# The v loads of three attention units, issued by GpSimd instead of the sync engine

## The chip, the core and the metric

The kernel runs on one core of one Trainium2 chip. The metric is the device time of one execution in microseconds; runs are given by their median.

## The reference

q, k and v have the shape (4, 8, 576, 64): batch, heads, sequence, head size. Attention is computed in chunks of 64 positions, each with itself alone. Its output goes through two MLPs; the result is float32.

```python
scores = scale * np.matmul(q_c, k_c.transpose(0, 1, 2, 4, 3))
attn = softmax(scores)
x = np.matmul(attn, v_c)                  # as (2304, 512)
x = ((x @ w_a) * (x @ w_b)) @ w_out       # 512 -> 1536 -> 512
h = x @ w_in                              # 512 -> 2048
P = a[0] + a[1] * h + a[2] * h**2 + a[3] * h**3
Q = 1.0 + abs(b[0]) * abs(h) + abs(b[1]) * h**2
out = (P / (Q + 1e-06)) @ w_out2          # 2048 -> 512
```

The weights arrive as 64-bit floats. The kernel loads each weight tile as it is (512 KB) and makes float32 of it on ScalarE and VectorE, in four pieces.

## The kernel before

The 2304 tokens are cut into 18 units of 128 (two chunks of 64, eight heads). A unit's attention runs in named pieces: `k` and `q` transpose the loaded k and q on TensorE (L359) and copy them out on ScalarE (L361); `S` makes the scores (L381), takes their maximum and subtracts it on VectorE (L386, L387); `X` is the exponential on ScalarE (L391); `E` normalizes on VectorE; `P` transposes the result (L407); `V` multiplies it with v (L425) and writes the upper part of x (`x_hi`); `L` makes the lower part (`x_lo`, L437). Matmuls are done as three products of such upper and lower parts (L275 to L277).

The kernel then goes through three stages: the gated product of the first MLP (first for units 0 to 2, while the other units' attention is woven in between; later for the rest), the product with `w_out`, and the second MLP with the rational function.

The order of everything is written out by hand. Two strings set the start: LOADS (L81) the DMAs and FIRST (L80) the compute pieces. A letter and a digit are a tensor or piece and its unit, `w` is the next weight tile or the next quarter of its conversion, `d` a few extra matmuls with the identity (L935), `+` a load.

```python
FIRST = "k0 q0 w w d2 S0 w X0 w k1 E0 d2 q1 S1 w X1 P0 k2 w q2 E1 V0 w S2 ...".split()
LOADS = "k0 q0 w k1 q1 w v0 k2 q2 v1 w w v2 k3 q3 k4 q4".split()
```

Each engine runs its instructions in program order. Loads are issued by the sync engine (SP), one after another; the stores of intermediate results go through GpSimd (POOL), whose first work is to make the identity matrix `ident` for the transposes. A load of q, k or v for a unit is 128 partitions by 8 heads by 64 floats: 1024 pieces of 256 bytes in the source, 256 KB in all. q, k and v of a unit up to unit 5 lie in one tile, `kqv`. Unit 0 to UH - 1 = 2 are the first three units, whose x the first gated matmuls read.

Of the kernel before, what the change touches and what calls it, by code (L numbers as in the profile page):

```python
# [20 lines left out]
def chunk_attention_two_mlps(  # L21
# [34 lines left out]
    nc = tc.nc  # L56
# [18 lines left out]
    UH = GH // P  # L75
# [248 lines left out]
    def a_load(u, *names):  # L324

        if u >= NU:
            return
        (b0, c0), (b1, c1) = CHUNKS[u]
        for nm, src in (("k", k), ("q", q), ("v", v)):
            if nm not in names:  # L330
                continue
            if u < 2 * UH:
                if ("raw", u) not in un:
                    un["raw", u] = p_X.tile([P, 3, H, D], F32, name="kqv", tag=f"X{NQ - 1}_{u + 1}")
                t = un["raw", u][:, "kqv".index(nm)]
            elif u % 2 and nm != "v":
                if nm == "k":
                    un["odd"] = p_X.tile([P, 3, H, D], F32, name="kq", tag=f"X{NQ - 1}_7")
                t = un["odd"][:, "kq".index(nm)]
            else:  # L340
                t = p_qk.tile([P, H, D], F32, name=nm, tag=nm, bufs=2 if nm == "v" else 1)
            if b0 == b1:
                parts = [(t, src[b0, :, c0 * CH:(c0 + 2) * CH, :])]
            else:
                parts = [
                    (t[c * CH:(c + 1) * CH], src[bb, :, cc * CH:(cc + 1) * CH, :])
                    for c, (bb, cc) in enumerate(((b0, c0), (b1, c1)))
                ]
            for dst, s in parts:
                nc.sync.dma_start(out=dst, in_=s.rearrange("h s d -> s h d"))  # L350
            raw[nm, u] = t

    def a_transpose(u, nm):
# [139 lines left out]
    def a_pv2(u):  # L493
# [31 lines left out]
        for n in (u + 2, u + 3):  # L525
            a_load(n, "v")
# [411 lines left out]
    for item in LOADS:  # L938
        if item == "w":
            w_fetch()  # L940
        else:
            a_load(int(item[1]), item[0])
# [3 lines left out]
    for item in FIRST:  # L946
        if item == "w":
            w_piece()
            continue
        if item[0] == "d":  # L950
            warm(int(item[1:]))
            continue
        if item[0] == "+":
            a_load(int(item[2]), item[1])
            continue
        a_piece(item[:-1], int(item[-1]))
# [228 lines left out]
```

## Time and profile before

| | us |
|---|---|
| median of 3 runs | 890.13 (889.49 to 890.37) |
| profiled execution | 888.48 |
| its span, first to last instruction | 886.7 |
| TensorE busy | 871.6 (98%) |
| VectorE busy | 716.8 (81%) |
| ScalarE busy | 609.9 (69%) |
| GpSimd busy | 64.1 (7%) |

The share of busy time is an average over the whole span. The rows below look at the start by itself: windows give the busy time of each engine in a stretch, the chain of waits follows the end of the stretch back to what released each step, and the waits name the DMA that an engine stood still for. `kqv<-in_v_dram` is a load of v, `q0 software_dynamic` the queue that GpSimd feeds and `q1 hardware_dynamic` the one that the sync engine feeds. The granted clock of TensorE is 1.00 in every window shown.

### The profile page before, as it was taken

The numbers are of one execution on the slowest core, as the hardware profiler recorded it, in microseconds if no ns is written. First come the engines' busy times: TensorE is split into PE (matmuls) and PEld (weight loads), VectorE is DVE, ScalarE is ACT, GpSimd is POOL, SyncE is SP. The second block draws the span as 40 slices with busy tenths as digits, with TensorE's granted clock in tenths as the row PEclk, the third lists the DMA queues.
The fourth block names the chain that finished last, engine by engine and source line by source line (L and its number), as shares of the span: only waits on it lengthen the run. The fifth ranks groups of instructions, "written<-read, shape, count | busy, mean of one in ns | idle before, by whom it ended". The sixth has DMA issues, their size and how long they took to land.

```text
span 886.7 us, 14668 instructions
## 1 busy us (share of the span) xinstructions
PE 871.6 (98%) x5528; PEld 782.5 (88%) x5528; DVE 716.8 (81%) x1252; ACT 609.9 (69%) x1088; POOL 64.1 (7%) x122
## 2 busy tenths in 40 slices
PE   5999999999999999999999999999999999999998
PEld 5899999999999999888888998888888888888997
DVE  6767887868887875578877799999889888988896
ACT  6867987445545543677886888876687767776875
POOL 0013111011111111000000000000000000000000
PEclk9999999999999999999999999999999999999999
DMA  9999984143434335578886200200020002000100
GB/s 232 256 271 315 269 230 155 66 143 125 148 126 134 118 124 173 160 245 284 284 272 215 72 1 1 83 1 1 1 95 1 1 1 84 0 1 1 49 1 36
DMA packets 107367, 105.82 MB, mean 119 GB/s; under 512 B 61472, under 2 KB 84512, under 8 KB 107296
## 3 DMA queue, kind: packets, MB, share of 16 engines
q1 hardware_dynamic: 99296, 79.71, 30.8%
q0 software_dynamic: 8000, 25.17, 7.6%
q8 instruction: 43, 0.70, 0.3%
q14 instruction: 28, 0.23, 0.1%
HBM read 74.98 MB, written 29.88 MB: 118 GB/s over the span
## 4 chain that ended last, share of the span: by engine, by line
PE 94%; DVE 2%; ACT 2%; issue 0%; DMA 0%; ACTq 0%; DVEq 0%
PE h L277 7%; PE h L275 7%; PE h L276 7%; PE acc L277 7%; PE acc L276 7%; PE acc L275 7%; PE acc L796 6%; PE acc L799 5%; PE acc L797 5%; PE ab L275 3%; PE ab L277 3%; PE ab L276 3%; PE y L275 3%; PE y L277 3%; PE y L276 3%; PE q L275 2%
## 5 line engine op out<-in xcount | busy, mean ns | idle before, releaser
L277 PE MATMUL h<-y,w_i 128*128 128x512 f32 (+1 forms) x320 | 117.7, 368 | 0.0
L275 PE MATMUL h<-y,w_i 128*128 128x512 f32 (+1 forms) x320 | 117.7, 368 | 0.0
L276 PE MATMUL h<-y,w_i 128*128 128x512 f32 (+1 forms) x320 | 117.6, 368 | 0.0
L854 ACT ACTIVATE a_ring<-h 128x512 f32<-128x512 f32 (+1 forms) x80 | 44.1, 552 | 85.7 <-PE h L277 85.7
L693 ACT COPY s<-y 128x384 f32<-128x384 f32 x72 | 34.7, 481 | 85.2 <-PE y L277 85.0
L796 PE MATMUL acc<-g_hi,w_o 128*128 128x512 f32 (+1 forms) x240 | 86.3, 367 | 0.0
L797 PE MATMUL acc<-g_hi,w_o 128*128 128x512 f32 (+1 forms) x240 | 86.2, 366 | 0.0
L857 DVE SCALAR_TENSOR_TENSOR u<-u,cb_t,a_ring 128x512 f32<-128x512 f32 (+1 forms) x80 | 55.6, 695 | 29.4 <-ACT u L855 28.7
L276 PE MATMUL acc<-w_o,g_hi 128*128 128x512 f32 x191 | 74.4, 390 | 0.0
L277 PE MATMUL acc<-w_o,g_lo 128*128 128x512 f32 x191 | 74.4, 389 | 0.0
L275 PE MATMUL acc<-w_o,g_hi 128*128 128x512 f32 x191 | 74.3, 389 | 0.0
L276 PEld LDWEIGHTS h<-y,w_i 128*128 128x128 f32 x320 | 60.1, 188 | 8.7
L275 PEld LDWEIGHTS h<-y,w_i 128*128 128x128 f32 x320 | 60.1, 188 | 8.6
L277 PEld LDWEIGHTS h<-y,w_i 128*128 128x128 f32 x320 | 60.1, 188 | 7.5
L776 DVE TENSOR_TENSOR g_lo<-g_raw,g_hi 128x512 fp32r<-128x512 f32 (+1 forms) x60 | 38.1, 636 | 28.5 <-ACT g_hi L774 13.6
L856 ACT ACTIVATE t<-h,ca_t 128x512 f32<-128x512 f32 (+1 forms) x80 | 59.1, 739 | 0.0
L799 PE MATMUL acc<-g_lo,w_o 128*128 128x512 f32 (+1 forms) x240 | 59.0, 367 | 0.0
L867 DVE SCALAR_TENSOR_TENSOR u<-u,r 128x512 f32<-128x512 f32 (+1 forms) x80 | 50.5, 631 | 9.2 <-ACT r L866 9.2
L859 DVE SCALAR_TENSOR_TENSOR t<-t,ca_t,h 128x512 f32<-128x512 f32 (+1 forms) x80 | 55.6, 695 | 2.8
L866 ACT ACTIVATE r<-r,nlsh 128x512 f32<-128x512 f32 (+1 forms) x80 | 54.6, 683 | 2.6
L607 POOL DMA_DIRECT2D g_d<-g x72 | 39.2, 545 | 232.4 <-DVE g L738 85.3
L865 ACT ACTIVATE r<-u,nlsh 128x512 f32<-128x512 f32 (+1 forms) x80 | 55.5, 694 | 0.5
(210 smaller groups left out, 2393.9 us busy)
## 6 DMA issues: line engine op xcount, KB each, us to landing
w_raw<-in_moe_w_out_dram SPq DMA_DIRECT2D x28, 512.0 KB, 3.9
g_d<-g POOLq DMA_DIRECT2D x72, 192.0 KB, 2.6
g_raw<-g_d SPq DMA_DIRECT2D x48, 256.0 KB, 4.0
w_raw<-in_moe_w_in_dram SPq DMA_DIRECT2D x16, 512.0 KB, 4.2
w_raw<-in_moe_w_a_dram SPq DMA_DIRECT2D x12, 512.0 KB, 6.1
w_raw<-in_moe_w_b_dram SPq DMA_DIRECT2D x12, 512.0 KB, 6.3
y_d<-ys POOLq DMA_DIRECT2D x16, 256.0 KB, 3.9
out_dram<-o SPq DMA_DIRECT2D x16, 256.0 KB, 2.3
```

Of the source, the lines that this page charges most:

```text
L275: nc.tensor.matmul(ps, wh, xh, start=first, stop=False, **kw)
L276: nc.tensor.matmul(ps, wh, xl, start=False, stop=False, **kw)
L277: nc.tensor.matmul(ps, wl, xh, start=False, stop=last, **kw)
L796: nc.tensor.matmul(acc[j][d], wh, gh, start=i == 0, stop=False)
L797: nc.tensor.matmul(acc[j][d], wl, gh, start=False, stop=False)
L799: nc.tensor.matmul(acc[j][d], cols(w, d)[0], gl, start=False, stop=i == F1 - 1)
L856: nc.scalar.activation(t, ps, AF.Identity, scale=ca_t[:, 3:4], bias=ca_t[:, 2:3])
L857: nc.vector.scalar_tensor_tensor(u, u, cb_t[:, 0:1], ah, ALU.add, ALU.mult)
L859: nc.vector.scalar_tensor_tensor(t, t, ca_t[:, 1:2], ps, ALU.add, ALU.mult)
L865: nc.scalar.activation(r, u, AF.Ln, scale=2.0 ** -LSH, bias=nlsh[:, 0:1])
L866: nc.scalar.activation(r, r, AF.Exp, scale=-1.0, bias=nlsh[:, 1:2])
L867: nc.vector.scalar_tensor_tensor(u, u, 1.0 + 1e-6, r, ALU.add, ALU.mult)
```

## The change

One line of `a_load` chooses the engine that issues a load. For v of units 0 to 2 that is now GpSimd; for all others it stays the sync engine.

```diff
             for dst, s in parts:
-                nc.sync.dma_start(out=dst, in_=s.rearrange("h s d -> s h d"))
+                (nc.gpsimd if nm == "v" and u < UH else nc.sync).dma_start(out=dst, in_=s.rearrange("h s d -> s h d"))
             raw[nm, u] = t
```

On the sync engine, the issues of the start before the change (`w_raw` is a weight tile, `kqv` the tile of a unit):

```order
L350 DMA kqv<-in_q_dram 128x8x64
L177 DMA w_raw<-in_moe_w_b_dram 128x4x256
L350 DMA kqv<-in_v_dram 128x8x64
L350 DMA kqv<-in_k_dram 128x8x64
L350 DMA kqv<-in_q_dram 128x8x64
L350 DMA kqv<-in_v_dram 128x8x64
L177 DMA w_raw<-in_moe_w_a_dram 128x4x256
L177 DMA w_raw<-in_moe_w_b_dram 128x4x256
L350 DMA kqv<-in_v_dram 128x8x64
L350 DMA kqv<-in_k_dram 128x8x64
```

and the same place after it:

```order
L350 DMA kqv<-in_q_dram 128x8x64
L177 DMA w_raw<-in_moe_w_b_dram 128x4x256
L350 DMA kqv<-in_k_dram 128x8x64
L350 DMA kqv<-in_q_dram 128x8x64
L177 DMA w_raw<-in_moe_w_a_dram 128x4x256
L177 DMA w_raw<-in_moe_w_b_dram 128x4x256
L350 DMA kqv<-in_k_dram 128x8x64
```

The three loads of v are gone and what stood behind each has moved up.

On GpSimd, where the identity is made and the first store of the gated product (`g_d`) follows, the difference is:

```order
 masks.py:199 ISA
 masks.py:199 AFFINE_SELECT ident<-ident 128x128
+L350 DMA kqv<-in_v_dram 128x8x64 x3
 L607 DMA g_d_83<-g 128x384
 L607 DMA g_d_84<-g 128x384
```

The three loads now stand directly behind the identity, with nothing to wait for.

## Rows read from the trace of the kernel before

**Rows 1.** Windows: busy us and instructions of PE, PEld, DVE, ACT, POOL; clock; DMA.

```profile
0.00:24.00 24.00, 14.74 (x255) 12.38 (x256) 15.25 (x33) 15.29 (x29) 0.70 (x6) 1.00 1.03 230
24.00:45.00 21.00, 19.86 (x238) 17.99 (x236) 16.56 (x33) 18.91 (x36) 1.22 (x2) 1.00 0.98 262
45.00:886.00 841.00, 837.02 (x5040) 752.15 (x5038) 684.99 (x1187) 575.68 (x1026) 62.15 (x114) 1.00 0.35 113
```

**Rows 2.** Chain of waits to 26 us: start us, us, what.

```profile
4.30 1.94 PE at L359 x8
...
8.23 0.70 DVE m L386
...
14.56 0.59 ACT t L361
...
15.15 0.52 ACT w_a L199
...
24.90 0.43 PE ab L276
```

**Rows 3.** Waits to 60 us: total us, times, longest us.

```profile
DVE w_a L237 <- DMA w_raw<-in_moe_w_a_dram: 6.2, 1, 6.2
...
PE at L359 <- DMA kqv<-in_k_dram: 5.1, 3, 4.3
...
PE at L359 <- DMA kqv<-in_q_dram: 0.5, 1, 0.5
```

**Rows 4.** Timeline of the sync queue: start us, us, what it issues.

```profile
1.86 1.04 SPq L177 DMA_DIRECT2D w_raw<-in_moe_w_a_dram  x1
...
3.50 0.95 SPq L350 DMA_DIRECT2D kqv<-in_q_dram  x1
```

**Rows 5.** Issue to landing of these two, in the same order.

```profile
DMA to landing us min/median/max: 5.2/5.2/5.2
...
DMA to landing us min/median/max: 5.9/5.9/5.9
```

**Rows 6.** Timeline of the engines: start us, us, engine, line, what.

```profile
1.02 0.29 POOL masks.py:199 TENSOR_SCALAR_AFFINE_SELECT ident<-ident 128x128 f32<-128x128 f32 x1
...
7.58 0.43 DVE L240 TENSOR_SCALAR w_a<-w_a 128x512 int32<-128x512 int32 x1
...
9.68 0.60 PE L359 MATMUL at<-ident,kqv 128*128 128x128 f32 x4
...
10.22 1.05 ACT L361 COPY t<-at 128x512 f32<-128x512 f32 x2
...
15.25 0.69 PE L425 MATMUL at<-pT,kqv 64*64 64x64 f32 x32
...
22.94 0.69 PE L425 MATMUL at<-pT,kqv 64*64 64x64 f32 x32 [0.32 <-ACT pT L409]
```

**Rows 7.** Windows of DMA activity; the last two columns are DMA share and GB/s.

```profile
2.50:3.50 1.00, 0.00 (x0) 0.00 (x0) 0.00 (x0) 0.00 (x0) 0.00 (x0) 1.00 1.22 277
...
20.00:23.00 3.00, 2.49 (x40) 2.07 (x31) 2.83 (x8) 2.89 (x7) 0.00 (x0) 1.00 0.91 195
...
51.90:52.10 0.20, 0.20 (x17) 0.13 (x9) 0.00 (x0) 0.00 (x0) 0.00 (x0) 1.00 1.04 417
```

**Rows 8.** DMA queues, 51.9 to 52.1 us: packets, MB, share of 16 engines.

```profile
q0 software_dynamic: 17, 0.08, 91.5%
q1 hardware_dynamic: 10, 0.01, 12.1%
```

**Rows 9.** GpSimd DMA of 156.54; DMA slices 156.4 to 157.8; landings, 156.54 and 32.29.

```profile
156.54 0.54 POOL L607 DMA_DIRECT2D g_d<-g  x1 [3.33 <-DVE g L611]
...
DMA  0000000000000000000000000000000000039997
...
DMA to landing us min/median/max: 2.1/2.1/2.1
...
DMA to landing us min/median/max: 6.5/6.5/6.5
```

## The prediction

> **What bounds the kernel now.** I read the windows first, then the chain of waits, the waits for DMAs, and the sync queue's issues beside their landings. The windows [rows 1] show two different kernels in one. From 45 us on TensorE is busy 837.02 of 841 us, so nothing there can absorb or return much. In the first 24 us it is busy 14.74 us: there the program waits for data and for short chains between engines. A microsecond lost or won before 24 us reaches the end at full size, unless what comes later was waiting for something else.
>
> The chain [rows 2] says what the start waits for. Behind the landing of k of unit 0 it goes to eight transposes from 4.30 without a break (k, then q of unit 0), to the scores, to VectorE's maximum at 8.23, and then through VectorE and ScalarE without any DMA up to the first gated matmuls at 24.90. The waits [rows 3] agree: in the first 60 us TensorE waits for k loads 5.1 us in 3 pieces, 4.3 of it at the start, and 0.5 us once for a q; VectorE waits 6.2 us for the first weight. Nothing waits for a v.
>
> **The change part by part.** Three DMAs of 256 KB leave the sync queue, where they stood seventh, tenth and thirteenth, and are issued by GpSimd behind the building of the identity. No arithmetic moves. Every later DMA of the sync queue stands one to three places earlier.
>
> *Removed from the sync queue:* its issue time, which nobody waits for. The first v is used at 15.25, the third at 22.94 [rows 6], and no wait there names a DMA, so an earlier v is worth nothing. What stood behind it could land earlier by one load. That is k and q of unit 2, on which TensorE waits 5.1 - 4.3 = 0.8 us at most and 0.5 us [rows 3]; I cost the gain at 0, since ScalarE, which copies these transposes out, runs from 14.56 into the weight cast behind it without a break in the chain [rows 2]. If that cover were not there, the gain would be at most 0.8 + 0.5 = 1.3 us.
>
> *Added on GpSimd:* three issues, from 1.02 + 0.29 = 1.31 us on [rows 6]. No wait is added in front of them. The next DMA of GpSimd comes at 32 us, far behind. A GpSimd DMA of 128 rows takes 0.54 us to write and 2.1 us to land in a quiet stretch [rows 9], with its first packets about 1.1 us after the issue: of the 40 slices from 156.4 to 157.8 the 36th is the first with any. So the first v starts to move near 2.4 us. A v load has 128 x 8 = 1024 pieces of 256 bytes and the trace has no such load from GpSimd: it is written in 0.54 us if the time is that of the instruction, in 8 x 0.54 = 4.3 us if it goes by pieces.
>
> *What the moved transfers push back* is the term that decides. At 2.5 to 3.5 us the DMA engines are carrying the first loads and are full: share 1.22 at 277 GB/s [rows 7]. One v is 262,144 bytes, so the three take 3 x 0.95 = 2.84 us at that rate; at 195 GB/s, the slow stretch, 4.03 us, and at 417 GB/s, the stretch where GpSimd's packets fill the engines, 1.89 us. Who goes first when both queues have work? In 51.9 to 52.1 us GpSimd's queue has a share of 91.5% and the sync queue 12.1% [rows 8]. So I take it that what GpSimd has written goes ahead of what the sync queue holds, and that until 10 us the three v delay all else by their own transfer time.
>
> What this costs depends on the slack of each load. k and q of unit 0: none, since TensorE starts on k as it lands and goes straight on to q [rows 2]. The first weight lands at 1.86 + 5.2 = 7.06 [rows 4, 5]; VectorE's second pass over it ends at 7.58 + 0.43 = 8.01 [rows 6] and the maximum follows at 8.23, so slack 0.2. q of unit 1 lands at 3.50 + 5.9 = 9.4, its transposes take 0.60, and its copy is the second of two that fill 10.22 to 11.27 on ScalarE, starting near 10.75 [rows 6]: slack 0.7. The delays don't add up; the largest one that is left after its slack shifts all that follows. If all three v pass before q of unit 0, the shift is 2.8 us. If two pass before the first weight is whole, 1.9 - 0.2 = 1.7. If all three pass before q of unit 1, 2.84 - 0.7 = 2.1. I take 2.3 us, between the first and the last and nearer to the last, as the third v can hardly overtake unit 0. Bounds of this term: 0.8 (slow writing, below) and 4.0 upwards; below zero, -1.3.
>
> How fast GpSimd writes many pieces is where the Trainium skill speaks: "DMA: Bandwidth & Descriptors", section "Anatomy of one DMA — SWDGE (gpsimd) path", says that one can emit a lot of descriptors before the added cost shows. By that rule the three loads would be written by 2.9 us and the shift would be the 2.8 us end; by the linear bound it would be the paced rival. No run here shows either yet.
>
> *The sum:* the profiled execution took 888.48 us with a span of 886.7; 888.48 + 2.3 = 890.8. It lies 1.65 us under the median of the runs shown, so on their scale 890.13 + 2.3 = 892.4 us.
>
> **The rivals.**
> 1. *Paced loads.* GpSimd needs 4.3 us for each, so that 2.84 us of transfers are spread over 13 us, 22% of the engines. Up to the first weight's landing that takes 0.22 x (7.06 - 2.4) = 1.0 us, less slack 0.2; up to q of unit 1, 0.22 x (9.4 - 2.4) = 1.5, less 0.7. Shift 0.8 us: 890.9. For it: eight times the pieces of any GpSimd DMA in the trace. Against it: the time shown, 0.54 us, is that of a whole instruction, of which the pieces may be a small part.
> 2. *Nothing is pushed back (the other side).* GpSimd's packets only use room that the sync queue leaves, as at 20 to 23 us with a share of 0.91 [rows 7]; the first v has from 2.4 to 15.25 to arrive. Then k and q of unit 2 come one load earlier and some of the 1.3 us of waits goes: -0.2 us as a value, 889.9, with -1.3 as its end. It decides when the first weight is delayed by less than its slack of 0.2. For it: the long time to the use of v. Against it: the shares in [rows 8] and the full engines at 2.5 to 3.5 us.
> 3. *Late v.* If VectorE keeps GpSimd from writing, a v comes after its use. VectorE's real work begins with the first weight, after 7.06, so at 4.3 us each only the second and third could be held up. The third would be written by 1.31 + 3 x 4.3 = 14.2, landed by 16.3 and is used at 22.94; it would have to lose over 6 us more before anything waits, and each microsecond beyond is one at the end, 894 and more. The GpSimd DMA at 32.29, in a stretch where VectorE is 79% busy (16.56 of 21 us), still lands in 6.5 us [rows 1, 9]. The rule is that of the Trainium skill, "SBUF — State Buffer", section "Who interferes with whom": descriptors from GpSimd starve while VectorE holds the shared port. By that row the time comes out as without it.
>
> **How the numbers follow.** Forecast 52%, paced 28%, nothing pushed back 17%, late v 3%. A measurement of this kernel can tell about 0.2%, 1.8 us, from no change. Of the forecast's 52 points 46 lie above +1.8 us and 6 under it, where the v transfers run at the 417 GB/s end. Paced gives 2 above and 26 within. The 17 of the second rival are 10 within and 7 faster; the -1.3 of its waits alone doesn't reach 1.8, so these 7 stand for what the rows can't show. Late v adds 3. Slower 51%, same 42%, faster 7%. The range runs from the second rival's value, 889.9, to 893.8, which is +3.7, most of the way to the 195 GB/s end; the forecast's own range is 891.8 to 893.8.
>
> **What would show it.** In the changed profile GpSimd has three DMAs near 1.3 us; their durations tell instruction time from time per piece. In the windows from 2.5 to 10 us the software queue should hold over half of the DMA share until its three loads are through. The first weight should land near 9.5 and VectorE wait over 8 us for it, or TensorE over 4.3 us for the first k. The first gated matmuls should stand in the chain near 27.2 instead of 24.90, and the chain be the same from there. It is wrong if the first weight lands before 7.3, if the shift at the first gated matmuls is regained before 45 us, or if anything waits for a v.

## The result and the profile after

The changed kernel takes 894.48 us (median of 4 runs, 893.71 to 895.05) against 889.81 us before on the same chip: ratio 1.0058, 95% interval 1.0046 to 1.0070 (the two medians alone give 1.0052). It is slower by 4.7 us, where 2.3 us were forecast and 893.8 us was the upper end of the range.

The windows of the changed profile answer to [rows 1]; columns as there:

```profile
0.00:24.00 24.00, 13.74 (x179) 11.66 (x182) 11.36 (x25) 11.95 (x21) 3.50 (x9) 1.00 1.07 231
...
45.00:886.00 841.00, 839.12 (x5071) 753.77 (x5063) 689.19 (x1196) 578.13 (x1030) 62.34 (x115) 1.00 0.35 112
```

From 45 us on TensorE works as before (839.12 of 841 us against 837.02). The loss lies ahead of 24 us, where it now works 13.74 instead of 14.74 us.

The chain of waits to 35 us answers to [rows 2] (start us, us, what):

```profile
2.86 8.80 DMA kqv<-in_k_dram
...
11.71 1.11 PE at L359 x4
...
12.83 0.85 PE at L935 x4
...
13.68 0.87 PE at L359 x4
...
14.57 0.59 ACT t L361
...
15.21 1.18 PE at L381 x32
...
16.41 0.70 DVE m L386
...
29.20 0.43 PE ab L276
```

The first piece of any length is now a DMA: k of unit 1, issued at 2.86, is there at 11.67. Before, this k was not in the chain at all. Behind it stand the extra matmuls, the transposes of q, the copy and the scores of unit 1, one after another without a gap. The second product of the first gated matmuls stands at 29.20 where it stood at 24.90: 4.30 us.

The waits to 60 us answer to [rows 3] (total us, times, longest us):

```profile
PE at L359 <- DMA kqv<-in_k_dram: 7.6, 2, 4.2
...
DVE w_a L237 <- DMA w_raw<-in_moe_w_a_dram: 7.3, 1, 7.3
```

TensorE waits for k loads 7.6 us in two pieces, 4.2 for the first as before and 3.4 for k of unit 1. VectorE gets the first weight 1.1 us later. No instruction waits for a v, and the one wait for a q of [rows 3] is gone from TensorE's matmuls. The first weight and q of unit 1 came from the sync queue as follows (start us and us of the issue, then issue to landing of the two in the same order):

```profile
1.86 0.96 SPq L177 DMA_DIRECT2D w_raw<-in_moe_w_a_dram  x1
...
3.41 0.98 SPq L350 DMA_DIRECT2D kqv<-in_q_dram  x1
...
DMA to landing us min/median/max: 6.3/6.3/6.3
...
DMA to landing us min/median/max: 9.5/9.5/9.5
```

So the first weight is there at 1.86 + 6.3 = 8.16 and q of unit 1 at 3.41 + 9.5 = 12.91, 3.5 us later than before; TensorE comes to this q only at 13.47.

What GpSimd does in this time, first on the timeline, then with the time from issue to landing (ns and us, min/median/max):

```profile
1.47 2.80 POOL L350 DMA_DIRECT2D kqv<-in_v_dram  x3 [0.16 <-issue]
```

```profile
L350 POOL DMA_DIRECT2D kqv<-in_v_dram x3: 882/894/1039, 1.5 to 3.4; - x3
...
DMA to landing us min/median/max: 5.2/7.9/8.4
```

The three loads are written in 0.88 to 1.04 us each, eight times the pieces of a load of [rows 9] in less than twice its time, and land 5.2 to 8.4 us after their issue.

The DMA queues of the changed kernel, from 4 to 5.5 us, 5.5 to 7 and 8 to 10.5 us (packets, MB, share of 16 engines):

```profile
q0 software_dynamic: 70, 0.25, 73.2%
...
q1 hardware_dynamic: 197, 0.08, 29.6%
...
q0 software_dynamic: 8, 0.00, 1.7%
...
q1 hardware_dynamic: 501, 0.46, 105.9%
...
q0 software_dynamic: 126, 0.41, 76.1%
...
q1 hardware_dynamic: 447, 0.11, 32.4%
```

and the sync queue before the change from 8 to 10.5 us:

```profile
q1 hardware_dynamic: 1384, 0.73, 113.6%
```

GpSimd's queue takes 73.2% and 76.1% of the engines in two bursts: v of unit 0 first, then the other two, with the first weight of the sync queue between them. In that gap, from 5.5 to 7 us, it moves 8 packets and the sync queue 501, though the instructions of all three loads had ended by 1.47 + 2.80 = 4.27; no run shows why it paused. Its packets are 0.41 MB / 126 = 3.3 KB on average in the second burst, the sync queue's 0.11 MB / 447 = 0.25 KB. So in 8 to 10.5 us the sync queue moves 0.11 MB instead of 0.73 MB, and it is k of unit 1 that stands there.

A measured shift needs one more number. The transposes of q of unit 1, which took 0.60 us [rows 6], and their neighbours on the changed kernel's timeline:

```profile
12.62 1.06 PE L935 MATMUL at<-ident 128*128 128x128 f32 x4
...
13.47 1.06 PE L359 MATMUL at<-ident,kqv 128*128 128x128 f32 x4
...
15.21 1.14 PE L381 MATMUL at<-t 64*64 64x64 f32 x32 [0.67 <-ACT t L361]
```

The same three, behind the transposes of k of unit 1, in the kernel before:

```profile
8.34 1.05 PE L359 MATMUL at<-ident,kqv 128*128 128x128 f32 x4 [0.18 <-DMA kqv<-in_k_dram]
...
9.23 0.61 PE L935 MATMUL at<-ident 128*128 128x128 f32 x4
...
9.68 0.60 PE L359 MATMUL at<-ident,kqv 128*128 128x128 f32 x4
...
11.32 0.69 PE L381 MATMUL at<-t 64*64 64x64 f32 x32 [1.05 <-ACT t L361]
```

Four transposes take 1.06 us where they took 0.60. These are durations of TensorE's two clock levels, 1.2 and 2.4 GHz: e2 and e4 below show the same instructions at 1.06 us with a granted clock of 0.50 and at about 0.6 us with 1.00. The clock column of the changed profile reads 1.00 here, but its first record stands at 20.5 us, so I go by the durations. In the kernel before the first record stands at 9.2 us, and by the durations the clock rose there, between the transposes of k and the extra matmuls: the 1.00 of its windows says nothing of the time ahead of that. In both kernels TensorE starts at the lower clock; behind its new pause the changed one stays there up to 20 us.

### The profile page after: what moved, and what is told of

It reads as the page before. It is cut to its first block, busy times and chain, and to the rows that moved or that the text cites. A ratio compares the mean times of both kernels' runs of the same rounds, so it can differ in the third digit from the quotient of the medians.

```text
span 892.2 us, 14671 instructions
## 1 busy us (share of the span) xinstructions
PE 874.9 (98%) x5528; PEld 784.9 (88%) x5528; DVE 716.8 (80%) x1252; ACT 609.9 (68%) x1088; POOL 66.8 (7%) x125
## 4 chain that ended last, share of the span: by engine, by line
PE 92%; ACT 3%; DMA 2%; DVE 2%; issue 1%; SPq 0%; ACTq 0%; DVEq 0%
PE h L275 7%; PE h L276 7%; PE h L277 7%; PE acc L276 7%; PE acc L275 7%; PE acc L277 7%; PE acc L796 5%; PE acc L797 5%; PE acc L799 5%; PE ab L275 3%; PE ab L277 3%; PE ab L276 3%; PE y L275 3%; PE y L276 3%; PE y L277 3%; PE q L275 2%
```

## The experiments

Start of three instructions in each profile's timeline, against the kernel before (us). "k1" is the first transpose of k of unit 1, "max 1" VectorE's maximum of unit 1's scores, "gated" the first gated matmul. The last column is the median time less that of the kernel before on the same chip (889.81 for the changed kernel, 889.03 for e1 to e4, 888.97 for e5 to e8).

| kernel | k1 | max 1 | gated | median |
|---|---|---|---|---|
| before | 8.34 | 12.11 | 24.48 | |
| changed | +3.37 | +4.30 | +4.30 | +4.67 |
| e1 held back | +0.51 | +1.44 | +1.77 | +3.2 |
| e2 sync queue alone | +3.84 | +4.77 | +5.02 | +4.0 |
| e3 v of unit 0 alone | +1.41 | +1.51 | +2.86 | +2.2 |
| e4 extra matmuls | +3.64 | +3.55 | +3.57 | +4.8 |
| e5 v of 1, 2 held back | +0.26 | +0.03 | +5.67 | +4.9 |
| e6 ScalarE's queue | +3.40 | +4.33 | +4.34 | +3.9 |
| e7 early matmuls, before | +0.28 | -0.13 | +0.92 | +0.7 |
| e8 earlier start, before | +0.40 | +0.21 | +0.20 | +0.7 |

Single executions of one kernel differ by up to 2 us (the kernel before: 888.32 to 890.47 in 21 runs), so a profile is read by its stages and a time by its median. A profile is one of these executions: that of e1 is the fastest of its five (890.71 us), that of e4 the slowest of its four (894.61).

**e1: GpSimd's loads held back.**

```diff
+            if nm == "v" and u < 2:
+                nc.gpsimd.tensor_copy(t[:, 0, 0:1], raw["q", u + 1][:, 0, 0:1])
             for dst, s in parts:
```

> The changed kernel, but GpSimd copies one column of q of unit 1 into the tile of v of unit 0 before it issues that load, and one column of q of unit 2 before v of unit 1, so its three loads start only when those q have landed. The sync queue is that of the changed kernel. Theory A (GpSimd's packets go ahead of the sync queue's and make k of unit 1 late): the k of unit 1 lands near 8.3 us as before the change, the first gated matmuls are within 0.5 us of before, time 889.3 to 890.5. Rival C (the loss comes from the sync queue's new order and waits, not from GpSimd's packets): k of unit 1 stays late and the time stays at 894.5.

Measured: 892.20 us, ratio 1.0035 (1.0022 to 1.0048). k of unit 1 is back near its old time (+0.51), as theory A says and rival C does not. But the time is not: 1.8 us at the first gated matmuls remain. The profile has two reasons that theory A didn't count, slow matmuls and, less, a wait for v of unit 1:

```profile
PE at L427 <- DMA kqv<-in_v_dram: 2.2, 1, 2.2
```

```profile
8.86 1.11 PE L361 MATMUL at<-ident,kqv 128*128 128x128 f32 x4 [0.74 <-DMA kqv<-in_k_dram]
...
10.62 1.06 PE L361 MATMUL at<-ident,kqv 128*128 128x128 f32 x4
```

The four transposes of q take 1.06 us, so +0.51 at k becomes +1.44 at the maximum; the wait for v of unit 1 takes it to +1.77. The expected time was wrong, the mechanism for k of unit 1 was not.

**e2: the same transfers in the sync queue alone.** The edit is to the kernel before.

```diff
-    LOADS = "k0 q0 w k1 q1 w v0 k2 q2 v1 w w v2 k3 q3 k4 q4".split()
+    LOADS = "k0 q0 v0 w v1 v2 k1 q1 w k2 q2 w w k3 q3 k4 q4".split()
```

> All loads in the sync queue, v of the first three units moved to where their transfers ran in the changed profile: k0 q0 v0 w v1 v2 k1 q1 w k2 q2 and so on. Theory A, the bytes ahead of k of unit 1 alone decide: three loads of 0.95 to 1.2 us each, k of unit 1 lands at 11.1 to 11.9, shift 3.5 to 4.7, time 893.3 to 894.5. Rival D (it is dearer on GpSimd's queue, because its packets of 4096 bytes hold an engine longer than the same bytes do in the sync queue): k of unit 1 lands before 10.8, time under 892.8.

Measured: 893.06 us, ratio 1.0045 (1.0029 to 1.0062). Without any load in GpSimd's queue, k of unit 1 is 3.84 us late, at 12.19, a little later than I expected, and the time a little under my range. Rival D falls: the bytes ahead of k of unit 1 decide, not the queue that they are in. The windows show the clock (the column of 0.50) where the transposes take 1.06 us:

```profile
12.00:20.00 8.00, 7.14 (x76) 6.29 (x79) 3.87 (x10) 4.03 (x8) 0.00 (x0) 0.50 1.07 288
```

```profile
12.19 1.11 PE L359 MATMUL at<-ident,kqv 128*128 128x128 f32 x4 [4.00 <-DMA kqv<-in_k_dram]
...
13.95 1.06 PE L359 MATMUL at<-ident,kqv 128*128 128x128 f32 x4
```

**e3: only v of unit 0 by GpSimd.**

```diff
-                (nc.gpsimd if nm == "v" and u < UH else nc.sync).dma_start(...)
+                (nc.gpsimd if nm == "v" and u < 1 else nc.sync).dma_start(...)
```

> Only v of unit 0 is loaded by GpSimd, v of units 1 and 2 stay in the sync queue. Theory A: the first weight lands near 8.2 us as in the changed kernel, which puts VectorE's first maximum 0.8 us later than before; k of unit 1 lands near 9.3, one load later, against a slack of 0.8; shift 0.8 to 1.3 us, time 890.6 to 891.1. Rival (any early load in GpSimd's queue brings the whole loss): 894.5. Rival C (order of the sync queue): one third of the loss, 891.4, with k of unit 1 on time.

Measured: 891.27 us, ratio 1.0024 (1.0012 to 1.0035), with runs in two groups, 889.3 to 890.5 and 892.0 to 892.8. k of unit 1 is one load late, +1.41, and the maximum of unit 1 +1.51: dose and loss go together, and one early load doesn't bring the whole loss. The time alone would suit rival C too (891.4), but that has k of unit 1 on time. The profiled run is of the slower group. Its shift grows from +1.5 to +2.86 between 19 and 25 us, where the granted clock is 0.50:

```profile
19.00:25.00 6.00, 5.24 (x52) 4.72 (x51) 5.67 (x14) 4.14 (x8) 0.00 (x0) 0.50 1.01 216
```

**e4: matmuls in TensorE's pause.**

```diff
-    FIRST = "k0 q0 w w d2 S0 w X0 w k1 E0 ...
+    FIRST = "k0 q0 w w d2 S0 w X0 w d8 k1 E0 ...
```

> The changed kernel with 8 extra matmuls with the identity in front of the transposes of k of unit 1, where TensorE stands still for 3.4 us. Theory B (about 1 us of the 4.3 us is TensorE's slower matmuls from 11.7 to 20.5 us, after the pause): transposes of four take about 0.6 us instead of 1.1, shift at the first gated matmuls 3.2 to 3.6 us, time 893.4 to 893.9. Rival (the late k alone is the whole loss): the shift stays 4.3 and the time 894.5, even if the matmuls are faster.

Measured: 893.79 us, ratio 1.0052 (1.0037 to 1.0067). The transposes take 0.63 us, and the first gated matmuls stand at +3.57 instead of +4.30, though k of unit 1 came 0.27 us later than in the changed kernel:

```profile
8.22 2.61 PE L935 MATMUL at<-ident 128*128 128x128 f32 x16
...
11.98 0.63 PE L359 MATMUL at<-ident,kqv 128*128 128x128 f32 x4 [1.15 <-DMA kqv<-in_k_dram]
...
13.60 0.63 PE L359 MATMUL at<-ident,kqv 128*128 128x128 f32 x4 [0.55 <-DMA kqv<-in_q_dram]
...
15.67 0.69 DVE L386 TENSOR_REDUCE m<-at 128x8 f32<-128x512 f32 x1 [0.96 <-PE at L381]
```

The window from 10 to 16 us, where the clock is 1.00, and the piece of the chain in front of the transposes of q:

```profile
10.00:16.00 6.00, 3.63 (x56) 2.95 (x54) 4.76 (x10) 3.97 (x7) 0.00 (x0) 1.00 1.20 244
```

```profile
3.36 10.11 DMA kqv<-in_q_dram
```

From this k to the maximum of unit 1 it takes 3.69 us, in the changed kernel 16.41 - 11.71 = 4.70. So about 1.0 us of the shift is the clock. More can't show here, because at the higher clock the chain goes through q of unit 1, for which TensorE waits 0.55 us. The time doesn't show the gain: against their own kernel before, e4 is 4.8 us slower and the changed kernel 4.7. In the profile of e4 some 2.5 us more are lost after 45 us, near 90 us, near 480 us and at the very end, for which I have no cause. So the clock's part is shown for this stage, not for the whole.

**e5: v of units 1 and 2 by GpSimd, behind q of unit 2.** v of unit 0 stays in the sync queue.

```diff
+            if nm == "v" and u == 1:
+                nc.gpsimd.tensor_copy(t[:, 0, 0:1], raw["q", u + 1][:, 0, 0:1])
-                (nc.gpsimd if nm == "v" and u < UH else nc.sync).dma_start(...)
+                (nc.gpsimd if nm == "v" and 0 < u < UH else nc.sync).dma_start(...)
```

> v of unit 0 stays in the sync queue at its old place; v of units 1 and 2 are loaded by GpSimd, which first copies one column of q of unit 2 and so waits until that q has landed (near 14 us). Theory A (only what passes ahead of k and q of units 0 to 2 costs): k of unit 1 lands as before, no wait for a v as v of unit 1 has to arrive by 19.6 us (GpSimd's load of the run held back to q of unit 1 took 7 us to land, so 20 to 21 us is possible, then up to 1 us is lost), TensorE's clock rises near 9 us as before; shift 0 to 1 us, time 889.0 to 890.0. Rival (a load of v in GpSimd's queue costs wherever it stands): 890.5 and more.

Measured: 893.83 us, ratio 1.0051 (1.0035 to 1.0066): my expectation was wrong. Up to the maximum of unit 1 nothing is lost (+0.03). Then the chain reads:

```profile
14.96 8.39 DMA kqv<-in_v_dram
...
23.49 1.13 PE at L427 x32
...
24.62 2.00 PE at L937 x8
...
26.62 0.85 PE at L409 x4
```

v of unit 1 takes 8.39 us from its issue, where e1's loads had taken 6.0 to 7.9 us. TensorE waits 5.48 us for it, and behind this pause the granted clock is 0.50, so that the gated matmuls come 5.67 us late:

```profile
23.00:28.00 5.00, 4.51 (x48) 4.43 (x48) 1.96 (x4) 2.35 (x5) 0.00 (x0) 0.50 0.75 224
```

Here the rival of the late v has happened, which I had at 3%.

**e6: ScalarE's hardware queue instead of GpSimd's.**

```diff
-                (nc.gpsimd if nm == "v" and u < UH else nc.sync).dma_start(...)
+                (nc.scalar if nm == "v" and u < UH else nc.sync).dma_start(...)
```

> The changed kernel with ScalarE's queue in the place of GpSimd's: the three v loads are issued from the beginning through a second hardware queue, with 256-byte packets as in the sync queue. Theory A in its form 'bytes ahead decide': the three loads share the engines packet by packet with the sync queue from 2 us on, all three are done by 8 us, and k of unit 1 lands 3 us late or more; time 892.5 to 894.5. Rival E (GpSimd's large packets push ahead and small ones would not): k of unit 1 at most 1.5 us late, time under 891.5.

Measured: 892.86 us, ratio 1.0042 (1.0029 to 1.0056). k of unit 1 is 3.40 us late, as with GpSimd (3.37). From 5 to 6.5 us this second queue, q10, has packets of 0.21 MB / 835 = 0.25 KB, as small as the sync queue's, and the larger part of the engines; from 4 to 5.5 us it is the other way round. The two windows in this order:

```profile
q10 hardware_dynamic: 835, 0.21, 87.2%
q1 hardware_dynamic: 449, 0.12, 47.8%
...
q1 hardware_dynamic: 857, 0.22, 87.5%
q10 hardware_dynamic: 506, 0.13, 46.6%
```

So the two queues take turns, and the third v landed at 11.9 us, not by 8 as I expected; k of unit 1 is late all the same. Rival E falls.

**e7 and e8: the kernel before, with an earlier start.**

```diff
-    FIRST = "k0 q0 w w d2 S0 w X0 w k1 E0 ...
+    FIRST = "d6 k0 q0 w w d2 S0 w X0 w k1 E0 ...            # e7
+    FIRST = "d6 k0 q0 d2 S0 w w X0 w w k1 E0 ...            # e8
-    LOADS = "k0 q0 w k1 q1 w v0 k2 q2 v1 ...
+    LOADS = "k0 q0 w k1 q1 w k2 q2 v0 v1 ...                # e8
```

> The kernel before the change, with 6 extra matmuls with the identity ahead of the first transposes, where TensorE waits for the first k from 1.4 to 4.3 us. Theory B on the clock: the granted clock rises earlier than at 9.2 us, the transposes and scores of unit 0 get shorter by about 1 us, but VectorE works on the first weight until 8.0 and takes the maximum only then, so the gain is at most 0.3 us: 888.7 to 889.1. Rival (the early matmuls at the lower clock are on the path for their whole length): 1 us faster, 888.0.

> The kernel before the change with the 6 extra matmuls at the start, the scores of unit 0 ahead of the first weight's conversion on VectorE and ScalarE, and k and q of unit 2 ahead of v of unit 0 in the sync queue. If the start is a chain in which each load's place decides, the first gated matmuls come 0.5 to 1.0 us earlier than before: time 888.0 to 888.6. If the chain is bound by ScalarE's own order from 10 us on: no change, 889.0.

Measured: e7 889.70 us, ratio 1.0006 (0.9997 to 1.0015), e8 889.66 us, 1.0009 (1.0000 to 1.0018). Neither gains. In e7 the clock is up by 7 us but falls again:

```profile
7.00:13.00 6.00, 3.72 (x80) 2.84 (x80) 5.39 (x11) 4.29 (x7) 0.00 (x0) 1.00 1.21 252
14.00:20.00 6.00, 5.81 (x80) 4.56 (x78) 4.51 (x10) 4.16 (x10) 0.00 (x0) 0.50 1.14 282
```

The maximum of unit 1 is 0.13 us earlier, that of unit 2 0.93 us later (17.90 against 16.97): with k of unit 2 landing only 0.14 us later, the lower clock costs about 1 us here. e8 has k and q of unit 2 transposed 0.6 and 0.9 us earlier and the first gated matmul 0.20 us later, with the clock at 1.00. Its maximum of unit 1 already stands at +0.21, and from there on nothing is gained. That is the test of the gain that the prediction set at 0: an earlier k or q of unit 2 is worth nothing here, as the chain through ScalarE [rows 2] suggests. No version beats the kernel before.

## Why the prediction was wrong

*What bounds the kernel* held. The start is a chain at full price: the shift is 4.30 us at 20 us and at the first gated matmuls. The profiled execution ends 5.5 us later. Of the other 1.2 us, 0.7 us come in a step between 400 and 480 us and 0.5 us at the very end, behind the last matmul. Steps up near 480 us are in e3 (about 1.5 us) and e4 (1.1 us) too and in none of the other profiles, so I don't put them to the change; their cause is open. The half microsecond at the end stands in the four profiles in which GpSimd issues two or three loads of v (the changed kernel, e1, e4 and e5: 0.4 to 0.5 us) and in none of the others, so it may belong to the change; no run shows how.

*Who goes first* held in part. While GpSimd's queue moves its packets it has 73 to 76% of the engines. But from 5.5 to 7 us it had 1.7%, so the sign "over half of the DMA share" up to the end of its three loads did not come, and only one v passed before the first weight. In e6 two queues take turns, in e2 there is only one, and k of unit 1 is as late in both: what costs is three more loads in front of it, on whichever queue.

*How fast GpSimd writes* came out near the quick end: 0.9 us a load, not 4.3. The paced rival falls. What the Trainium skill says in "DMA: Bandwidth & Descriptors", section "Anatomy of one DMA — SWDGE (gpsimd) path", of emitting a lot of descriptors agrees with this trace: 1024 pieces were written in 0.88 to 1.04 us. The rule of the Trainium skill about starved descriptors ("SBUF — State Buffer", section "Who interferes with whom"), which stood behind the late v, is not seen at work in any run here: see e5's row below.

*The step that failed* is "If all three v pass before q of unit 1, 2.84 - 0.7 = 2.1. I take 2.3 us". The case was the right one, but the shift was 4.30 us, above the 4.0 that the prediction gave as the upper bound of this term. Both of its terms were off, in one direction, and a third one, the clock, was left out:

- The transfer. Three loads at 277 GB/s were 2.84 us. k of unit 1 starts 3.37 us late, which is 786,432 bytes at 233 GB/s, or 1.12 us a load. I had taken the rate of a stretch without a second queue. The bounds, 1.9 to 4.0 us, held it.
- The load and its slack. The prediction asked for the slack of q of unit 1 and took off 0.7 us, but k of unit 1 stands in front of q, in the queue and on TensorE, and TensorE had waited 0.18 us for it before. q was 3.5 us late itself, but when TensorE came to it at 13.47 it was there. Behind k about 0.4 us are free (an estimate: 1.36 us of slower steps, below, less the 0.93 us that came on top).
- The clock, put at nothing. TensorE stands still for 3.4 us and goes on at its lower clock. The extra matmuls and the transposes of q then take about 0.45 us more each, and the scores 1.14 us instead of 0.69: 1.36 us in all. The slack is used up and 0.93 us come on top. 3.37 + 0.93 = 4.30 us. e2 and e6, with the same slow transposes, show the same 0.93 us between k of unit 1 and the maximum (3.84 to 4.77, 3.40 to 4.33); e4, with the fast ones, shows none (3.64 to 3.55). Durations of a row were taken for the changed kernel, without asking at which clock it would run after a new wait.

*The first weight* was expected near 9.5 and landed at 1.86 + 6.3 = 8.16, since only v of unit 0 went ahead of it; VectorE waited 7.3 us for it, not over 8. The chain didn't pass through it. The gated matmuls were expected in the chain near 27.2 and stand at 29.20. None of the three signs of being wrong showed, so they didn't cover a start that loses more than forecast without waiting for a v.

*The rivals.* The sync queue's loads were pushed back and nothing was gained, so the second falls; e8 shows that its gain isn't there even with k and q of unit 2 early. No v was late in the changed kernel. e5 shows that a v can be late. The reason given for that rival isn't seen: the instructions of the two loads took 0.9 to 1.0 us each beside a VectorE that was busy 5.50 of 6 us:

```profile
15.00:21.00 6.00, 2.52 (x74) 2.02 (x72) 5.50 (x13) 4.69 (x10) 1.90 (x2) 1.00 1.17 266
```

And in the changed kernel GpSimd's loads took 5.2 to 8.4 us to land, though VectorE did nothing between 0.9 and 8.2 us, so a busy VectorE isn't needed for a slow load. What a load waits for after its instruction has ended, no run here tells apart. In e5 GpSimd's queue begins to move about 3 us after the issue, and a few packets come late.

## What to carry to other kernels

When the DMA engines are full, as in the start of this kernel, a second queue doesn't add a lane, it changes the order: what it carries delays what the first queue holds (3.37 us with GpSimd's queue, 3.40 with ScalarE's, 3.84 with the same loads moved forward in the sync queue). Move there only what is needed before the loads that it will pass, and ask for the slack of the next load in line, not for that of the load that moved. A wait that is new to TensorE can cost more than its own length, because the steps behind it may run at the lower clock (3.37 us became 4.30 here); slack read off at the full clock can be used up by that. A load that is held back until nearly the time of its use has to be given the landing time of a busy stretch, not that of a quiet one (e1, e5).

## What the runs showed of the hardware

- A GpSimd load of 1024 pieces is written in 0.88 to 1.04 us, one of 128 rows in 0.54 us.
- GpSimd's loads took 5.2 to 8.4 us from issue to landing in the changed kernel and 6.0 to 8.4 us in e1 and e5, while the sync queue was full, as against 2.1 us in a quiet stretch [rows 9]; held back until they were nearly needed, as in e1 and e5, they were the ones that were late.
- With loads of 256-byte pieces in the sync queue, GpSimd's queue (3.3 KB a packet on average) had 73 to 76% of the engines while it moved, and 1.7% in the 1.5 us between its two bursts.
- The runs of e3 lie in two groups 2 us apart. In the profile, which is of the slower group, 1.3 us are lost at a clock of 0.50 between 19 and 25 us and about 1.5 us in a step near 480 us. The mean granted clock of each run doesn't part the groups (0.999 to 1.000 in the faster, 0.996 to 1.000 in the slower), so what does is open.
